# Linear attention and a bilinear layer on one core: SBUF tiles sorted into four pools by their role on TensorE

## The chip, the cores and the metric

The kernel runs on one core of a Trainium2 chip. A core has TensorE (PE, the matrix engine), VectorE (DVE), ScalarE (ACT), GpSimd (POOL) and SyncE (SP, which issues most DMAs here). SBUF is the on-chip memory of 128 partitions from which the engines read, PSUM the one that TensorE writes. The metric is the device time of one execution, in microseconds, as the median of several; less is better.

## The reference

Two stages are computed, all in float32: linear attention with positive random features, then a bilinear layer over the joined heads.

```python
scale = 1.0 / np.sqrt(np.sqrt(D))                    # 8 batches, 8 heads, 576 tokens, D = 64
def phi(x):                                          # omega: 128 features
    proj = np.einsum('bhsd,md->bhsm', x, omega)
    h = proj - np.sum(x * x, axis=-1, keepdims=True) / 2.0
    return np.exp(h - np.max(h, axis=-1, keepdims=True)) / np.sqrt(m)
q_p, k_p = phi(q * scale), phi(k * scale)
kv, z = np.einsum('bhsm,bhsd->bhmd', k_p, v), np.sum(k_p, axis=2)
num = np.einsum('bhsm,bhmd->bhsd', q_p, kv)
attn = num / (np.einsum('bhsm,bhm->bhs', q_p, z)[..., None] + 1e-06)
x = attn.transpose(0, 2, 1, 3).reshape(B * S, H * D) # 4608 tokens of 512
out = (x @ w_a) * (x @ w_b) @ w_out                  # 512 -> 1536 -> 512
```

## The kernel before

The bilinear layer's matmuls keep float32's accuracy by splitting each operand in two halves of a shorter float type (F32R), one rounded and one rest. A product of two matrices is then three matmuls for each 128 rows that are summed over: rounded by rounded, rounded by rest, rest by rounded. In one matmul one operand is *stationary* (it is loaded into the array first, by LDWEIGHTS, 128 columns) and the other *moving* (it is streamed through, 256 or 512 columns). Each matmul here has a load of its own, and the load for the next matmul is under way while the one before it streams.

The first two blocks of 512 tokens go plainly, in `moe_block`: L1319 multiplies a weight tile (stationary, names `w`, `wa`, `wb`) by x (moving, 512 columns). From block 2 on, `moe_block7` saves an eighth of the products by Strassen's scheme (Winograd's form): weights and x are added in advance (`t` tiles from DRAM, `Sa` and `Sb`), and each *unit* is seven products of six matmuls at L1410, with 256 moving columns. Their results stand in two PSUM banks `p0` and `p1`, which VectorE drains with an addition into `c` at L1420. The output matmuls are L1129 (`ghl` stationary, `wo` moving, 512 columns) and, in the last two blocks, L1198 (256 columns, with `ghl` or the sums `og` stationary and `wo` or the sums `ot` moving). The attention of the later heads runs in *bursts* between the units, as packed small fp32 matmuls: L633 (projections, `om` moving, `X` stationary), L910 (keys by values) and L982 (queries by `k`).

The order of everything is set by a planner (class `Graph`) ahead of time. It gives each buffer a *slot* of a ring; slots such as `u0` to `u11`, `x0` to `x3` or `wo0` to `wo2` are the unit of allocation, and several buffers use one slot one after another (`t` lies in `u2` to `u6`, `bq` in `a0` and `a1`, `ot` in `X0`, `X1`, `hq1` and `qd0`, `og` in `nat` and `ht` slots). The function `alloc` turns a slot into an address: it asks a pool for a tile with the slot as its tag, and the pool lays tags out one behind the other in the order in which they are first asked for.

Of the kernel before, what the change touches and what calls it, by code (L numbers as in the profile page):

```python
# [15 lines left out]
X = mybir.AxisListType.X  # L16
# [45 lines left out]
class Buf:  # L62
# [7 lines left out]
    def part(self, k):  # L70
        return self, k
# [311 lines left out]
def tile_attention_moe(ctx: ExitStack, tc: tile.TileContext, kqt, kqtt, kqn, kqnt, vx, omst, idn, wab, wout, out):  # L383
    nc = tc.nc
    SQPE = CFG["SQPE"]
    const = ctx.enter_context(tc.tile_pool(name="const", bufs=1))
    sp = ctx.enter_context(tc.tile_pool(name="sp", bufs=1))
    ps = ctx.enter_context(tc.tile_pool(name="ps", bufs=1, space=PSUM))
    dram = ctx.enter_context(tc.tile_pool(name="dram", bufs=1, space=bass.MemoryType.DRAM))
    wide = wab.dtype == I64  # L390
# [6 lines left out]
    for name, n in dict(X=2, Xw=0, nat=2, x2=0, v=1, xg=1, hk=1, hq=3, qd=1, kvz=0, sm=3, sq=3, ht=3, Xt=1, xl=0, xts=2, rd=2, x=4, xa=2, xf=2, Sa=2, Sb=2, st=0,  # L397
                        w=NF // 2, rw=0, u=NF, t=0, tst=0, wo=3, raw=2, a=2, c=0, bq=0, ghl=2, osb=0, ot=0, owr=0, og=0, ogf=0, oc=0, zs=1, z2=1, zb=2, k2=4, dn=1, tails=0, zq=2, zx=2,
# [7 lines left out]
                oc=["v0", "xg0", "Xt0", "raw0", "raw1"])  # L406
    PS = {"at", "ab", "o"}

    def alloc(b):
        pool = ps if b.ring in PS else sp  # L410
        b.ap = pool.tile(b.shape, b.dtype, tag=b.slot, name=b.name)

    def fixed(shape, dtype, name):
# [27 lines left out]
    for k in range(4):  # L441
        g.op({"POOL": 110}, lambda e, k=k: nc.gpsimd.memset(ind.ap[D * (k // 2):D * (k // 2) + D, D * (k % 2):D * (k % 2) + D], SQ2 * (k in (0, 3))),
             w=[(ind, k)], alloc=[ind] if k == 0 else [], prio=-5000)
# [55 lines left out]
    for kind, i, ws in units:  # L499
        n = place[kind, i, ws[0]]  # L500
# [1034 lines left out]
    with tc.manual_schedule():  # L1535
        for o in order:
            for b in o.alloc:
                alloc(b)
            o.fn(next(iter(o.eng)))
# [74 lines left out]
```

## Time and profile before

| | us |
|---|---|
| median of 3 runs | 1033.49 (1033.02 to 1034.39) |
| profiled execution, its own time | 1033.61 |
| its span, which the profile covers | 1031.8 |
| TensorE busy in the span | 1021.0 |
| VectorE busy | 876.7 |
| ScalarE busy | 575.5 |
| GpSimd busy | 109.1 |

The profiled execution's own time is 1.8 us longer than the span: what lies before the first and after the last instruction of the profile. Matmuls are pipelined, so a matmul's duration (281 ns in the mean for 256 columns) is far longer than the step from its start to the next one's start; the text calls that step the pace. "Busy" joins overlapping matmuls, so that a window that begins at one matmul's start and ends at a later one's start reads as busy throughout if nothing is missing between them, and its length divided by the matmuls that start in it is the pace. The count in brackets after a busy time also counts matmuls that only reach into the window.

### The profile page before, as it was taken

Reading aid. Unit: us, or ns where it says so; the run is one execution under the profiler, and the core shown is the slowest. Engines: PE = TensorE matmul, PEld = TensorE weight load, DVE = VectorE, ACT = ScalarE, POOL = GpSimd, SP = SyncE. Lnnn points to the kernel's source line nnn. Section 1 sums busy time; section 2 is a strip of 40 time slices with the busy share of each in tenths; the row PEclk is TensorE's granted clock in tenths of the full one; section 3 lists DMA queues with packets and bytes.
Section 4 is the critical chain, followed back from the end, with each engine's and each line's share of the span. In section 5 each row is a group of like instructions: output and inputs, shape, how many; then the busy total and the mean of one; then the engine's idle time right before and its main releaser. Section 6 shows DMA issues by size and latency. Waiting matters only on the chain.

```text
span 1031.8 us, 27457 instructions
## 1 busy us (share of the span) xinstructions
PE 1021.0 (99%) x10538; PEld 902.8 (87%) x10538; DVE 876.7 (85%) x2162; ACT 575.5 (56%) x1584; POOL 109.1 (11%) x157
## 2 busy tenths in 40 slices
PE   9999999999999999999999999999999999999998
PEld 7777777777798989989998988988998999999998
DVE  6999999899997979877996889888877578999776
ACT  7998897667755647655663566475454024232221
POOL 0221222101111111111110111111110000000000
PEclk9999999999999999999999999999999999999999
DMA  9778877998899988999899989988887889999991
GB/s 353 292 254 258 283 247 244 309 327 303 297 318 375 323 293 296 339 307 298 276 314 339 301 272 321 334 261 299 280 297 251 279 297 332 307 348 334 366 322 43
DMA packets 123428, 306.76 MB, mean 297 GB/s; under 512 B 17952, under 2 KB 41248, under 8 KB 123296
## 3 DMA queue, kind: packets, MB, share of 16 engines
q1 hardware_dynamic: 122416, 304.34, 86.1%
q8 instruction: 83, 1.36, 0.5%
q10 hardware_dynamic: 880, 0.66, 0.2%
q14 instruction: 49, 0.40, 0.1%
HBM read 249.60 MB, written 55.34 MB: 296 GB/s over the span
## 4 chain that ended last, share of the span: by engine, by line
PE 91%; DVE 6%; ACT 2%; issue 1%; DVEq 0%; ACTq 0%
PE p L1410 40%; PE o L1129 23%; PE pb L1319 5%; PE pa L1319 5%; PE o_P L1198 5%; PE pkv L910 3%; PE ppk L633 3%; PE p L633 2%; PE p L982 2%; DVE sm L659 1%; DVE raw L482 1%; PE p L1198 1%; PE ppq L633 1%; PE pm L982 1%; ACT hk L672 0%
## 5 line engine op out<-in xcount | busy, mean ns | idle before, releaser
L1420 DVE TENSOR_TENSOR c<-p,c 128x512 f32<-128x512 f32 (+1 forms) x336 | 208.6, 621 | 72.1 <-PE p L1410 68.4
L1129 PE MATMUL o<-wo,ghl 128*128 128x512 f32 x1008 | 258.3, 397 | 0.0
L1129 PEld LDWEIGHTS o<-wo,ghl 128*128 128x128 f32 x1008 | 181.4, 188 | 39.7 <-issue 5.0
L1410 PE MATMUL p<-x,w 128*128 128x256 f32 x1008 | 136.5, 281 | 0.2
L1410 PEld LDWEIGHTS p<-x,w 128*128 128x128 f32 x1008 | 131.0, 188 | 6.5 <-DVE c L1420 0.6
L1410 PE MATMUL p<-Sa,t 128*128 128x256 f32 x1008 | 133.1, 281 | 0.0
L1410 PEld LDWEIGHTS p<-Sa,t 128*128 128x128 f32 x1008 | 125.5, 188 | 0.1
L424 ACT COPY c<-p 128x256 f32<-128x256 f32 x84 | 31.0, 369 | 121.6 <-PE p L1410 108.5
L940 ACT ACTIVATE hq<-hq,dn 128x128 f32<-128x128 f32 x224 | 69.7, 391 | 29.2 <-DVE dn L936 28.9
L857 POOL TENSOR_TENSOR z<-hk 128x256 f32<-128x256 f32 x28 | 24.4, 870 | 532.7 <-ACT hk L672 458.9
L1410 PE MATMUL p<-x,t 128*128 128x256 f32 x504 | 73.2, 281 | 0.8 <-DVE oc L1208 0.8
L1410 PE MATMUL p<-Sb,t 128*128 128x256 f32 x504 | 73.5, 282 | 0.0
L1410 PE MATMUL p<-Sb,bq 128*128 128x256 f32 x504 | 73.3, 281 | 0.0
L930 DVE CUSTOM_DVE_ANT_0 zero<-hq,zb 128x128 bf16<-128x128 f32 x224 | 68.8, 307 | 4.1
L672 ACT ACTIVATE hq<-hq,sm 128x128 f32<-128x128 f32 x196 | 64.8, 393 | 7.4 <-DVE sm L667 7.3
L1410 PEld LDWEIGHTS p<-x,t 128*128 128x128 f32 x504 | 66.1, 188 | 2.1 <-DVE oc L1208 1.0
L672 ACT ACTIVATE hk<-hk,sm 128x128 f32<-128x128 f32 x188 | 61.3, 393 | 8.2 <-DVE sm L667 8.1
L1410 PEld LDWEIGHTS p<-Sb,t 128*128 128x128 f32 x504 | 65.7, 189 | 0.0
L1410 PEld LDWEIGHTS p<-Sb,bq 128*128 128x128 f32 x504 | 65.5, 188 | 0.1
L432 DVE TENSOR_TENSOR ghl<-c,ghl 128x512 fp32r<-128x512 f32 (+1 forms) x86 | 54.2, 643 | 5.1 <-ACT ghl L424 4.5
L424 ACT CAST ghl<-c 128x512 fp32r<-128x512 f32 (+1 forms) x60 | 32.9, 566 | 45.8 <-PE o L1129 28.0
L1470 DVE TENSOR_TENSOR c<-c,c 128x512 f32<-128x512 f32 x82 | 55.5, 711 | 0.8
(245 smaller groups left out, 1903.6 us busy)
## 6 DMA issues: line engine op xcount, KB each, us to landing
t<-td SPq DMA_DIRECT2D x168, 512.0 KB
wo<-wod SPq DMA_DIRECT2D x96, 512.0 KB
bq<-bd SPq DMA_DIRECT2D x84, 256.0 KB
qdr<-qd SPq DMA_DIRECT2D x112, 144.0 KB
hq<-qdr SPq DMA_DIRECT2D x28, 576.0 KB
X<-in_kqt_dram SPq DMA_DIRECT2D x30, 512.0 KB
td<-ts SPq DMA_DIRECT2D x24, 512.0 KB
v<-in_vx_dram SPq DMA_DIRECT2D x28, 288.0 KB
```

Source lines behind the costliest of these rows:

```text
L424: nc.scalar.copy(o(), i())
L432: return lambda e: ENG[e].tensor_tensor(o(), i(), f(hi()), op=ALU.subtract)
L633: nc.tensor.matmul(flat4(pps[w])[half, c * M:c * M + M], x()[rows, c * P:c * P + P][:, half], om.ap[rows], start=True, stop=True)
L672: g.op({"ACT": 393 if b >= B1 or not own else 359}, lambda e, c=c, w=w, to=to, at=at: nc.scalar.activation(to.ap[:, at + c], src[w](c), AF ...
L930: g.op({"DVE": 302}, lambda e, c=c, qc=qc: nc.vector.tensor_tensor_reduce(out=junk.ap[:], in0=qc(), in1=zb.ap[:], scale=1.0, scalar=0.0, o ...
L940: g.op({"ACT": 392}, lambda e, c=c, src=src: nc.scalar.activation(hq.ap[:, c], src(), AF.Copy, scale=dn.ap[:, c:c + 1]), r=[sd, (dn, None) ...
L1129: nc.tensor.matmul(po.ap[:], ghl.ap[:, gi, t * P:(t + 1) * P], wo.ap[:, wi], start=(n == 0 and i == 0), stop=(n == NF - 1 and i == 2))
L1198: nc.tensor.matmul(pb.ap[:, t], A[0](ai)[:, t * P:(t + 1) * P], W[0](wi), start=begin and t == j == 0, stop=stop and t == 1 and j == 2)
L1319: nc.tensor.matmul(pb.ap[:], wt.ap[:, wi, c], xs[c].at(xi), start=(c == 0 and i == 0), stop=(c == NC4 - 1 and i == 2))
L1410: nc.tensor.matmul(pb.ap[:, half], wcol(wi, c), xc(xi, c), start=n == 0, stop=n == 5)
L1420: g.op({"DVE": dve(n)}, lambda e: nc.vector.tensor_tensor(c4.ap[:, o], pb.ap[:, half], y(), op=ALU.add), r=[*((pb, k) for k in range(half. ...
L1470: g.op({"DVE": dve(SM)}, lambda e, v=v, C=C: nc.vector.tensor_tensor(v(C[1]), v(C[1]), v(C[0]), op=ALU.mult), r=part, w=part[2:], prio=-10)
```

## The change

One SBUF pool becomes four, and `alloc` chooses by the slot's name.

```diff
-    sp = ctx.enter_context(tc.tile_pool(name="sp", bufs=1))
+    sp = [ctx.enter_context(tc.tile_pool(name=f"sp{k}", bufs=1)) for k in range(4)]
...
+    STATIONARY, SHIM, MOVING = ("w", "u", "a", "ghl", "wo", "nat", "ht", "hk0", "hq0"), ("sm0",), ("x", "xa", "xf", "Sa", "Sb", "X", "qd", "hq1")
+
+    def part(slot):
+
+        names = (slot, slot.rstrip("0123456789"))
+        return next((k for k, part in enumerate((STATIONARY, SHIM, MOVING)) if any(n in part for n in names)), 3)
+
     def alloc(b):
-        pool = ps if b.ring in PS else sp
+        pool = ps if b.ring in PS else sp[part(b.slot)]
         b.ap = pool.tile(b.shape, b.dtype, tag=b.slot, name=b.name)
```

Pool 0 takes the slots that hold stationary operands, pool 2 those that hold moving ones, pool 3 the rest. Pool 1 holds one tile of 192 bytes, `sm0`; it stands between pools 0 and 2 and shifts the second against the first. Tiles of pools 0 and 2 are multiples of 256 bytes long, so that each pool has one offset modulo 256. The order of the instructions on every engine, the tiles that they name and the semaphores that they wait for are the same in both programs, row for row; only addresses move. Nothing is added and nothing is left out.

These are the offsets modulo 256 of the tiles that the four lines read, as both programs' allocations give them:

| slots (what lies in them) | before | now |
|---|---|---|
| `w0` to `w5` (weights) | 32, 64, 96, 128 | 64 |
| `u0` to `u11` (weights, `t`, in some blocks two of the x) | 0, 64, 128, 160, 192 | 64 |
| `a0`, `a1` (`bq`) | 32, 96 | 64 |
| `ghl0`, `ghl1` | 64, 192 | 64 |
| `wo0` to `wo2`, `hk0`, `hq0` (`wo`) | 0, 128, 160, 192 | 64 |
| `nat`, `ht` (`og`) | 0, 96, 160 | 64 |
| `x0` to `x3`, `xa0`, `xa1` | 0, 96, 128, 160, 192 | 0 |
| `Sa`, `Sb` | 128, 192 | 0 |
| `X0`, `X1`, `hq1`, `qd0` (`ot`) | 32 | 0 |
| `om` (pool `const`, moving in L633) | 192 | 192 |

A matmul's *distance* is the offset of its moving tile less that of its stationary tile, modulo 256; the parts of a tile that single matmuls read lie multiples of 256 bytes apart. By the allocations the matmuls of each line stand at these distances:

| line (matmuls in the program) | before | now |
|---|---|---|
| L1410 (3528) | 0: 732, 32: 564, 64: 468, 96: 426, 128: 396, 160: 120, 192: 444, 224: 378 | 192: 3312, 0: 216 |
| L1198 (510) | all eight, 12 to 150 each | 192: 264, 0: 246 |
| L1129 (1008) | 0: 168, 64: 336, 128: 168, 192: 336 | 0: 1008 |
| L1319 (576) | all eight, 45 to 108 each | 192: 576 |
| L633 (1080, fp32) | 160: 1008, others: 72 | 192: 896, 160: 112, 128: 72 |
| L910 (1008, fp32) | 160: 896, 224: 64, 64: 48 | 192: 1008 |

## Rows read from the trace of the kernel before

**Rows 1.** The page: its span, the busy engines, the chain by engine and line.

```profile
span 1031.8 us, 27457 instructions
...
PE 1021.0 (99%) x10538; PEld 902.8 (87%) x10538; DVE 876.7 (85%) x2162; ACT 575.5 (56%) x1584; POOL 109.1 (11%) x157
...
PE 91%; DVE 6%; ACT 2%; issue 1%; DVEq 0%; ACTq 0%
PE p L1410 40%; PE o L1129 23%; PE pb L1319 5%; PE pa L1319 5%; PE o_P L1198 5%; PE pkv L910 3%; PE ppk L633 3%; PE p L633 2%; PE p L982 2%; DVE sm L659 1%; DVE raw L482 1%; PE p L1198 1%; PE ppq L633 1%; PE pm L982 1%; ACT hk L672 0%
```

**Rows 2.** Windows of 50 us, all engines.

```profile
core 0: us, PE busy (x) PEld busy (x) DVE busy (x) ACT busy (x) POOL busy (x), PEclk, DMA share, GB/s
...
850.00:900.00 50.00, 48.98 (x387) 47.29 (x386) 45.11 (x97) 17.07 (x38) 0.00 (x0) 1.00 0.90 317
900.00:950.00 50.00, 50.00 (x426) 50.00 (x425) 47.44 (x99) 17.21 (x39) 0.00 (x0) 1.00 0.95 342
950.00:1000.00 50.00, 50.00 (x426) 50.00 (x425) 37.18 (x74) 11.15 (x29) 0.00 (x0) 1.00 0.95 347
```

**Rows 3.** Waits of PE from 200 us to the end.

```profile
PE ppq L633 <- issue: 1.5, 1, 1.5
PE p L1410 <- DVE oc L1208: 0.8, 1, 0.8
```

**Rows 4.** Windows over 114 runs of L1410, their sum.

```profile
sum 404.84, PE 404.60 PEld 403.97 DVE 334.05 ACT 188.29 POOL 37.08; mean PE 3.55 PEld 3.54 DVE 2.93 ACT 1.65 POOL 0.33
```

**Rows 5.** Windows over products of L1410, sums at distances 0, 32, 96, 192.

```profile
sum 32.87, PE 32.87 PEld 32.85 DVE 26.02 ACT 16.31 POOL 4.53; mean PE 0.71 PEld 0.71 DVE 0.57 ACT 0.35 POOL 0.10
...
sum 42.96, PE 42.96 PEld 42.93 DVE 38.91 ACT 18.23 POOL 4.37; mean PE 0.70 PEld 0.70 DVE 0.64 ACT 0.30 POOL 0.07
...
sum 38.88, PE 38.88 PEld 38.73 DVE 32.55 ACT 13.44 POOL 4.08; mean PE 0.72 PEld 0.72 DVE 0.60 ACT 0.25 POOL 0.08
...
sum 21.70, PE 21.70 PEld 21.69 DVE 17.20 ACT 8.90 POOL 1.56; mean PE 0.70 PEld 0.70 DVE 0.55 ACT 0.29 POOL 0.05
```

**Rows 6.** Fourth to sixth start in those products: distance 192, then 0.

```profile
881.93:882.16 0.24, 0.24 (x4) 0.24 (x3) 0.24 (x2) 0.00 (x0) 0.00 (x0) 1.00 1.11 443
...
958.35:958.59 0.24, 0.24 (x4) 0.24 (x3) 0.00 (x0) 0.00 (x0) 0.00 (x0) 1.00 1.15 460
...
sum 7.08, PE 7.08 PEld 7.08 DVE 5.33 ACT 2.41 POOL 0.66; mean PE 0.23 PEld 0.23 DVE 0.17 ACT 0.08 POOL 0.02
...
sum 10.99, PE 10.99 PEld 10.99 DVE 8.01 ACT 5.53 POOL 1.30; mean PE 0.24 PEld 0.24 DVE 0.17 ACT 0.12 POOL 0.03
```

**Rows 7.** Windows over three steps of L1129, sums at distances 0, 64, 128, 192.

```profile
sum 31.77, PE 31.77 PEld 25.98 DVE 25.40 ACT 15.40 POOL 3.45; mean PE 0.69 PEld 0.56 DVE 0.55 ACT 0.33 POOL 0.08
...
sum 56.81, PE 56.81 PEld 46.32 DVE 49.91 ACT 25.50 POOL 8.25; mean PE 0.69 PEld 0.56 DVE 0.61 ACT 0.31 POOL 0.10
...
sum 33.46, PE 33.46 PEld 27.14 DVE 31.54 ACT 21.73 POOL 7.57; mean PE 0.70 PEld 0.57 DVE 0.66 ACT 0.45 POOL 0.16
...
sum 66.46, PE 66.46 PEld 53.62 DVE 62.94 ACT 34.69 POOL 7.85; mean PE 0.70 PEld 0.56 DVE 0.66 ACT 0.37 POOL 0.08
```

**Rows 8.** Windows over three steps of L1319, 147 windows, all distances.

```profile
sum 102.35, PE 102.35 PEld 82.74 DVE 97.43 ACT 79.97 POOL 23.96; mean PE 0.70 PEld 0.56 DVE 0.66 ACT 0.54 POOL 0.16
```

**Rows 9.** Windows over 35 runs of L1198, their sum.

```profile
sum 55.96, PE 55.96 PEld 55.96 DVE 49.56 ACT 14.36 POOL 0.00; mean PE 1.60 PEld 1.60 DVE 1.42 ACT 0.41 POOL 0.00
```

**Rows 10.** Timeline of one drain, start and length: VectorE, then PE.

```profile
408.51 0.69 DVE L1420 TENSOR_TENSOR c<-p,c 128x512 f32<-128x512 f32 x1
...
409.72 0.87 PE L1410 MATMUL p<-x,t 128*128 128x256 f32 x6
```

**Rows 11.** Groups of instructions: VectorE differences of 128x512.

```profile
L432 DVE TENSOR_TENSOR ts<-tf,ts 128x512 fp32r<-128x512 f32 x24 | 16.1, 677 | 0.2 <-DMA td<-ts 0.2
L432 DVE TENSOR_TENSOR Sa<-st,Sa 128x512 fp32r<-128x512 f32 x14 | 10.0, 719 | 1.2 <-ACT Sa L424 1.2
```

**Rows 12.** Groups of instructions: one of L1410.

```profile
L1410 PE MATMUL p<-Sa,t 128*128 128x256 f32 x1008 | 133.1, 281 | 0.0
```

## The prediction

> **What bounds the kernel now.** I read the page first. TensorE is busy 1021.0 us of a span of 1031.8, VectorE 876.7 [rows 1]. The reader is to see that no engine but TensorE is near the span. Then the chain that ended last: the four lines of split-float matmuls (L1410, L1129, L1319, L1198) make 79% of the span, and the fp32 matmuls (L910, L633, L982) about 12% [rows 1]. [...] Last the waits of PE from 200 us to the end: two, 2.3 us in all [rows 3]. So PE is the bound because it works without a break, and the time can only fall if the break-free stream itself gets shorter: by fewer matmuls, or by a shorter pace from one matmul to the next. The change leaves every instruction, its order and its waits as they are. What is left is the pace.
>
> **What the pace depends on in this trace.** The pace is the step from one matmul's start to the next one's. Over the 114 unbroken runs of L1410 it takes 404.84 us for 3414 steps from one start to the next [rows 4]; less the 0.8 us of the one wait [rows 3] that is 118.3 ns. This is not one number. In the code each product is six matmuls; where both its pairs of tiles have the same distance (moving address minus stationary address, modulo 256, from the allocation), I put a window from its first start to the next product's start, and summed the windows by distance. There are 46, 61, 54 and 31 of them for distances 0, 32, 96 and 192; the other four distances lie between these. The sums [rows 5] divided by six times these counts give 119.1, 117.4, 120.0 and 116.7 ns. The instructions are the same in each, only the addresses differ, so the distance seems to move the pace, and 192 is the best.
>
> A product is too short to show what 192 does when it lasts: the step just before it had another distance. So I took the two steps from the fourth to the sixth start. For 192 they take 7.08 us over 31 windows, 62 steps: 114.2 ns. For 0 they take 10.99 us over 46 windows, 92 steps: 119.5 ns [rows 6]. In four of the 31 windows the two steps take 0.235 to 0.24 us (two of the four are in group 6), about 118 each; in the other 27 then (7.08 - 4 x 0.236) / 54 = 113.6. I keep this second rhythm in mind as a rival.
>
> For 512 columns I took steps of three matmuls. L1129 has 46, 82, 48 and 95 of them undisturbed, for distances 0, 64, 128 and 192: 230.2, 231.0, 232.3 and 233.2 ns, 231.9 over all [rows 7]. L1319 has 147 at 102.35 us, 232.1 ns [rows 8]. There 0 is best and 192 worst, so one distance is not best for both shapes.
>
> **The change, term by term.** By the new addresses, 3312 of the 3528 matmuls of L1410 stand at 192 and 216 at 0 (the first product of each unit in batches 3, 5 and 7, whose x lies in u slots); of L1198 264 at 192 and 246 at 0; all 1008 of L1129 at 0; all 576 of L1319 at 192.
> - L1410 at 192: 3312 x (118.3 - 114.2) = 13.6 us less. L1198 at 192: its pace now is 55.96 us over 475 steps in 35 runs, 117.8 ns [rows 9]; 264 x 3.6 = 1.0 us less.
> - Each run still has to settle. A whole product at 192 takes 116.7 a step against 114.2 in its later part, so an entry costs 6 x 2.5 = 15 ns. With 114 runs of L1410 and 36 units that start at 0 that is 150 x 15 = 2.2 us more.
> - At 0: (216 + 246) x (119.5 - 118.3) = 0.6 us more.
> - L1129: 1008 x (231.9 - 230.2) = 1.7 us less. L1319: 576 x (233.2 - 232.1) = 0.6 us more, by the row of L1129 at 192.
> - The sum of these is 14.6 - 2.2 - 0.6 + 1.7 - 0.6 = 12.9 us less.
> - Waits. A shorter PE stream meets the engines that drain its banks. A typical loop: VectorE's addition from 408.51 for 0.69 us ends at 409.20, and the product that writes this bank again starts at 409.72 [rows 10], 0.52 us later; the 12 matmuls between the bank's last product and that start take about 12 x 4.1 = 50 ns less, a tenth of this slack. The tight place is 850 to 950 us, where PE has its one wait for VectorE (L1208) and VectorE has 7.5 us free in 100. PE's 387 + 426 matmuls there, nearly all of 256 columns, get 813 x 4.1 = 3.3 us shorter, so more than half of VectorE's free time remains. I take 1 us of new waits; bounds 0 and 5 (next part).
> - At nothing: the other engines' addresses. VectorE's 128x512 differences from SBUF take 677 and 719 ns in two groups whose tiles lie at different offsets [rows 11], 6% apart at most by addresses. VectorE has 155 us free over the span [rows 1], which covers 17% on every one of its instructions; only in 850 to 950 us, with 7.5 us free, would 8% be too much, and each per cent over it costs 1 us. The fp32 matmuls: L910 goes from distance 160 to 192, L633 mostly too. No row shows them at 192. The best and the worst distance of 256 columns are 114.2 and 120.0, -3.5% to +1.4% of 118.3; on 12% of the span (124 us) that is -4.3 to +1.7 us. I take 0, inside these bounds, as no row is nearer.
>
> So 12.9 - 1 = 11.9 us less than the profiled execution's 1033.61, of which 1031.8 is the span: 1021.7. The median of the runs shown is 1033.49, 0.1 lower, so **1021.6**.
>
> [...]
>
> **The rivals.**
> - *No effect.* The distances in the trace go with tiles, and tiles with places in a unit; if the place sets the pace, new addresses change nothing: 1033.5. Against it: the 31 windows at 192 are of three kinds of product (x by w, x by t, Sb by t), lie between 294 and 992 us, and each kind has windows of 0.23 us. [...] 7%.
> - *The slow rhythm.* If the long runs lock into the rhythm of the four slow windows, 118.0 ns, L1410 gains 3312 x 0.3 = 1.0, L1198 loses 0.1, and with +1.7, -0.6 and -0.6 about 1.5 us are left: 1032. For it: four of 31, and nothing in the rows says what starts it. 8%.
> - *Another bound.* From 850 to 1000 us the DMA share is 0.90 to 0.95, and VectorE is at 95% in 900:950 [rows 2]. If nothing is gained there, 1239 matmuls x 4.1 = 5 us come back: 1026.6. Against it: PE has no wait for a DMA now [rows 3], and 3.5% on a share of 0.95 stays below 1. 7%.
> - *Slower: the fp32 matmuls.* L910 and L633 move to a distance that no row shows. It decides from 11.9 + 2.1 = 14 us, 11% on their 124 us; at 12.5% it would be 15.5 us, 1037. The whole spread over distances, 114.2 to 120.0, is 5%, so this needs twice what distance does anywhere in the trace. 6%, with whatever else new addresses may slow.
>
> **Chances and range.** The forecast has 72%. What a measurement of this kernel can tell from no change is 0.2%, 2.1 us. Faster: 72 + 7, and a little of the slow rhythm, 0.80. Same: no effect and most of the slow rhythm, 0.14. Slower 0.06. The best case has every step at 113.6 (2.1 us more), no entry cost (2.2), no new wait (1) and part of the 4.3 us on the fp32 matmuls: 1014. Upward the range takes in the other bound and the slow rhythm: 1032; no effect and slower are left out, 13%. The forecast's own range is 1015 to 1026.
>
> **What will show it.** The sums over L1410's runs: 114.5 to 115.5 ns a step instead of 118.3, and a mean of PE's 256-column matmuls under the present 281 ns [rows 12]. L1129 near 230, L1319 no better than now. PE's waits after 200 us at 2 to 4 us. Wrong would be: steps at 118 in long runs (slow rhythm), unchanged sums (no effect), more than 5 us of PE waits for VectorE or DMA (another bound), or L910 and L633 longer by more than 5 us.

## The result, and the profile after

The changed kernel takes 1024.66 us (median of four, 1024.24 to 1026.86) against 1033.94 for the kernel before beside it (1033.02 to 1036.25): a ratio of 0.9911, 95% interval 0.9889 to 0.9933, 9.3 us less. The forecast was 1021.6 with a range of 1014 to 1032, and faster at 0.80. Side and range hold; the gain is 9.3 us where 11.9 were forecast. The profiled execution took 1024.62 us, its span is 1022.7: 9.1 us less than before. Lines of the changed kernel are 7 higher: L1417 is L1410 of before, L1136 L1129, L1326 L1319, L1205 L1198, L640 L633, L917 L910.

First the page: span, busy engines, and one group of matmuls; they answer to [rows 1] and [rows 12].

```profile
span 1022.7 us, 27457 instructions
...
PE 1010.7 (99%) x10538; PEld 893.0 (87%) x10538; DVE 875.7 (86%) x2162; ACT 575.4 (56%) x1584; POOL 109.9 (11%) x157
...
L1417 PE MATMUL p<-Sa,t 128*128 128x256 f32 x1008 | 130.0, 278 | 0.0
```

The counts are those of before. PE's busy time falls by 10.3 us and VectorE's by 1.0: PE still has hardly a gap (12.0 us of the span without work, 10.8 before), and its stream has become shorter. The windows of [rows 2]:

```profile
850.00:900.00 50.00, 48.84 (x403) 47.53 (x402) 45.58 (x97) 17.05 (x37) 0.00 (x0) 1.00 0.92 323
900.00:950.00 50.00, 50.00 (x434) 49.85 (x433) 46.75 (x97) 16.15 (x37) 0.00 (x0) 1.00 0.95 345
950.00:1000.00 50.00, 50.00 (x440) 50.00 (x439) 38.67 (x77) 11.03 (x28) 0.00 (x0) 1.00 0.91 339
```

Where 1239 matmuls stood in these 150 us, 1277 stand now, at the same granted clock of 1.00. VectorE did not become the bound, and the DMA share stayed at or under 0.95. The waits of PE from 200 us on, as in [rows 3]:

```profile
PE ppq L640 <- issue: 1.5, 1, 1.5
PE p L1417 <- DVE oc L1215: 0.9, 1, 0.9
```

2.4 us against 2.3. The next rows are sums of windows over unbroken runs of one line, from a run's first start to its last. First L1417 (114 runs, 3414 steps) and L1205 (35 runs, 475 steps), to set beside [rows 4] and [rows 9]; then L1136 (130 runs, 878 steps) and L1326 (39 runs, 537 steps).

```profile
sum 397.39, PE 397.10 PEld 396.35 DVE 332.00 ACT 186.49 POOL 37.71; mean PE 3.48 PEld 3.48 DVE 2.91 ACT 1.64 POOL 0.33
...
sum 55.29, PE 55.29 PEld 55.29 DVE 49.55 ACT 14.71 POOL 0.00; mean PE 1.58 PEld 1.58 DVE 1.42 ACT 0.42 POOL 0.00
...
sum 204.77, PE 204.77 PEld 168.65 DVE 185.28 ACT 114.97 POOL 26.18; mean PE 1.58 PEld 1.30 DVE 1.43 ACT 0.88 POOL 0.20
...
sum 129.95, PE 128.98 PEld 102.93 DVE 123.76 ACT 105.47 POOL 28.16; mean PE 3.31 PEld 2.64 DVE 3.17 ACT 2.70 POOL 0.72
```

The kernel before has no row yet for the last two; the same runs there (L1129, then L1319):

```profile
sum 206.98, PE 206.98 PEld 168.83 DVE 186.79 ACT 115.35 POOL 26.39; mean PE 1.59 PEld 1.30 DVE 1.44 ACT 0.89 POOL 0.20
...
sum 128.16, PE 127.89 PEld 103.02 DVE 122.43 ACT 104.01 POOL 28.78; mean PE 3.28 PEld 2.64 DVE 3.14 ACT 2.67 POOL 0.74
```

So L1417 gains 404.84 - 397.39 = 7.45 us, L1205 0.67, L1136 2.21, and L1326 loses 1.79 (0.70 of that is idle PE: 129.95 - 128.98 against 128.16 - 127.89). Together 8.5 of the span's 9.1 us lie inside these runs; the rest lies in what is between them. L1417's mean step is 397.39 / 3414 = 116.4 ns. The prediction wanted 114.5 to 115.5.

Undisturbed steps, in windows of three as in [rows 7] and [rows 8]: L1136 in two sums of 135 windows, then L1326 in one of 146.

```profile
sum 92.75, PE 92.75 PEld 75.78 DVE 86.72 ACT 55.18 POOL 16.87; mean PE 0.69 PEld 0.56 DVE 0.64 ACT 0.41 POOL 0.12
...
sum 92.48, PE 92.48 PEld 76.20 DVE 80.62 ACT 42.19 POOL 10.70; mean PE 0.69 PEld 0.56 DVE 0.60 ACT 0.31 POOL 0.08
...
sum 102.19, PE 102.19 PEld 82.07 DVE 96.79 ACT 80.89 POOL 22.91; mean PE 0.70 PEld 0.56 DVE 0.66 ACT 0.55 POOL 0.16
```

185.23 / 810 = 228.7 ns for L1136 (231.9 before) and 102.19 / 438 = 233.3 for L1326 (232.1 before).

**Two rhythms.** To see why L1417 stays above 115.5, I cut each run of 12 or more matmuls that follows L1136 and holds no step above 126 ns (72 runs) at its tenth start, and summed what is left by two things: the distance of the run's first product, and the last step of L1136 ahead of it (the time from its last start to the run's first). The four sums: first product at 0, last step under 233 ns (17 runs, 496 steps); at 0, 233 or more (5 runs, 112 steps); at 192, under 233 (44 runs, 1012 steps); at 192, 233 or more (6 runs, 90 steps).

```profile
sum 56.22, PE 56.22 PEld 56.22 DVE 45.03 ACT 28.43 POOL 7.26; mean PE 3.31 PEld 3.31 DVE 2.65 ACT 1.67 POOL 0.43
...
sum 12.70, PE 12.70 PEld 12.70 DVE 12.31 ACT 10.59 POOL 0.50; mean PE 2.54 PEld 2.54 DVE 2.46 ACT 2.12 POOL 0.10
...
sum 118.80, PE 118.80 PEld 118.80 DVE 93.72 ACT 54.01 POOL 13.50; mean PE 2.70 PEld 2.70 DVE 2.13 ACT 1.23 POOL 0.31
...
sum 10.32, PE 10.32 PEld 10.32 DVE 9.56 ACT 5.32 POOL 3.08; mean PE 1.72 PEld 1.72 DVE 1.59 ACT 0.89 POOL 0.51
```

The quotients are 113.35, 113.4, 117.4 and 114.7 ns. Window by window there is almost nothing in between: the steps that are summed are all at distance 192, and a run goes at about 113.3 (fast) or at about 117.7 ns (slow) to its end. Twelve of these late parts, nine of them among the 44, are only two steps long. All 22 runs that start at 0 are fast. Of the 50 that start at 192, 42 are slow: 41 of 44 after a short last step of L1136, one of 6 after a long one. The slow rhythm of the prediction's rival is real. A batch is here, as in the prediction, one of the blocks of 512 tokens, counted from 0: 32 of these 42 lie in batches 2, 4 and 6, where no unit starts at 0, and the other ten, in batches 3 and 5, begin with a later product of a unit. In batch 8 no unit starts at 0 either, but its runs follow L1205 and not L1136, and they go at 55.31 us over 485 steps, 114.0 ns.

### The profile page after: what moved, and what is told of

Same layout as the page of the kernel before. It is cut to its first block, busy times and chain, and to the rows that moved or that the text cites. A ratio compares the mean times of both kernels' runs of the same rounds, so it can differ in the third digit from the quotient of the medians.

```text
span 1022.7 us, 27457 instructions
## 1 busy us (share of the span) xinstructions
PE 1010.7 (99%) x10538; PEld 893.0 (87%) x10538; DVE 875.7 (86%) x2162; ACT 575.4 (56%) x1584; POOL 109.9 (11%) x157
## 4 chain that ended last, share of the span: by engine, by line
PE 86%; DVE 8%; DMA 2%; ACT 2%; issue 1%; SPq 0%; ACTq 0%; DVEq 0%
PE p L1417 39%; PE o L1136 21%; PE o_P L1205 5%; PE pa L1326 5%; PE pb L1326 4%; PE pkv L917 3%; PE ppk L640 2%; PE p L640 2%; PE p L989 2%; DVE raw L489 1%; DVE sm L666 1%; DMA X<-in_kqt_dram 1%; PE p L1205 1%; PE ppq L640 1%; ACT hk L679 1%
## 5 line engine op out<-in xcount | busy, mean ns | idle before, releaser
L1136 PE MATMUL o<-wo,ghl 128*128 128x512 f32 x1008 | 255.5, 395 | 0.0
L1136 PEld LDWEIGHTS o<-wo,ghl 128*128 128x128 f32 x1008 | 181.0, 188 | 38.0 <-issue 4.8
L1417 PE MATMUL p<-x,w 128*128 128x256 f32 x1008 | 135.7, 281 | 0.3
L1417 PEld LDWEIGHTS p<-x,w 128*128 128x128 f32 x1008 | 130.0, 189 | 6.4 <-DVE c L1427 0.9
L1417 PE MATMUL p<-Sa,t 128*128 128x256 f32 x1008 | 130.0, 278 | 0.0
L1417 PEld LDWEIGHTS p<-Sa,t 128*128 128x128 f32 x1008 | 122.4, 188 | 0.1
L1417 PE MATMUL p<-x,t 128*128 128x256 f32 x504 | 72.6, 280 | 0.9 <-DVE oc L1215 0.9
L1417 PE MATMUL p<-Sb,bq 128*128 128x256 f32 x504 | 71.9, 279 | 0.0
L1417 PE MATMUL p<-Sb,t 128*128 128x256 f32 x504 | 71.8, 278 | 0.0
L1417 PEld LDWEIGHTS p<-x,t 128*128 128x128 f32 x504 | 65.4, 188 | 2.3 <-DVE oc L1215 1.1
L1417 PEld LDWEIGHTS p<-Sb,bq 128*128 128x128 f32 x504 | 64.5, 188 | 0.1
L1417 PEld LDWEIGHTS p<-Sb,t 128*128 128x128 f32 x504 | 64.3, 188 | 0.0
```

The costliest lines, as they stand in the source:

```text
L1136: nc.tensor.matmul(po.ap[:], ghl.ap[:, gi, t * P:(t + 1) * P], wo.ap[:, wi], start=(n == 0 and i == 0), stop=(n == NF - 1 and i == 2))
L1417: nc.tensor.matmul(pb.ap[:, half], wcol(wi, c), xc(xi, c), start=n == 0, stop=n == 5)
```

## The experiments

Twelve runs. Eleven are of the changed kernel with tiles sorted otherwise and the instructions of every engine in the same order (ten kernels, one of them run twice), one is of the changed kernel itself. The kernel before ran beside them in three groups (medians 1034.65, 1034.22 and 1034.20). "DISTANCE", "LOCK" and so on are the names of the theories in the expectations.

**Distance 0.** The 192 bytes between pools 0 and 2 are taken away.

```diff
-    STATIONARY, SHIM, MOVING = (...), ("sm0",), ("x", ...)
+    STATIONARY, SHIM, MOVING = (...), (), ("x", ...)
```

> The changed kernel without the 192 bytes between pools 0 and 2: all 3528 matmuls of L1417, all of L1205 and all 576 of L1326 stand at distance 0, L1136 stays at 0; the fp32 lines move too (L917 from 192 to 0, L640 mostly from 192 to 128). Theory DISTANCE (the pace goes with moving less stationary address modulo 256): L1417 and L1205 at 119 to 120 ns a step instead of 116.4, 4038 x 3.1 = 12.5 us more; L1326 at 229 like L1136 instead of 233.3, 576 x 4.3 = 2.5 us less; 1024.7 + 10 = 1034.7. Rival SORTING (the gain comes from tiles of one role lying together, not from the distance): 1024.7, L1417 at 116.4.

1037.11 us, ratio to before 1.0029 (1.0014 to 1.0044): about 12 us above the changed kernel, and slower than before by 0.3%. Sums over L1417's 114 runs, then over 146 windows of three steps of L1326:

```profile
sum 409.82, PE 409.65 PEld 409.01 DVE 336.53 ACT 189.32 POOL 37.50; mean PE 3.59 PEld 3.59 DVE 2.95 ACT 1.66 POOL 0.33
...
sum 99.71, PE 99.71 PEld 82.17 DVE 95.58 ACT 80.07 POOL 22.26; mean PE 0.68 PEld 0.56 DVE 0.65 ACT 0.55 POOL 0.15
```

409.82 / 3414 = 120.0 ns for L1417, and 99.71 / 438 = 227.6 for L1326. Both go the way that the distance says, in opposite directions in the one kernel. SORTING falls: tiles lie sorted by role here too, and the gain is gone. The forecast was 2.4 us low; L1417 went 0.5 ns above the 119.5 that was assumed. L1205's 35 runs take 56.99 us, 120.0 ns a step, as forecast.

**All tiles moved by 192 bytes, distances kept.** A tile of 192 bytes ahead of pool 0.

```diff
-    STATIONARY, SHIM, MOVING = ("w", ...), ("sm0",), ("x", ...)
+    FRONT, STATIONARY, SHIM, MOVING = ("sm1",), ("w", ...), ("sm0",), ("x", ...)
```

> A tile of 192 bytes ahead of pool 0: every tile of the four pools moves by 192 bytes (stationary offset 64 to 0, moving 0 to 192), all distances of the split-float lines stay; only L640, whose om lies outside the pools, goes from distance 192 to 0. Theory DISTANCE: 1024.7, within 1 us, L1417 at 116.4 and with the same slow and fast stretches. Rival ADDRESS (each tile's own offset counts, not the difference): L1417 leaves 116.4, anything up to the 118.6 of before, up to 1032. If fp32 matmuls minded their distance it would show in L640 alone.

1023.91 us (1021.70 to 1025.07), ratio 0.9899 (0.9882 to 0.9915), the same as the changed kernel's within the intervals. L1417's runs:

```profile
sum 397.61, PE 397.33 PEld 396.64 DVE 331.69 ACT 186.29 POOL 37.60; mean PE 3.49 PEld 3.48 DVE 2.91 ACT 1.63 POOL 0.33
```

397.61 against 397.39 us. ADDRESS falls as far as one such move can show it: every tile's own offset has changed, the differences have not, and the pace stays. The two rhythms come back too: cut as above, all 43 stretches of L1417 that start at 192 after a short last step are in the slow rhythm, and none of the 7 after a long one.

**The other distances.** 32, 64, 128, 160 and 224 bytes between the pools, by other small tiles in the place of `sm0`.

```diff
-    ... ("sm0",) ...
+    ... ("rd0",) ...             32 bytes
+    ... ("zq0",) ...             64
+    ... ("zx0",) ...             128
+    ... ("zx0", "rd0") ...       160
+    ... ("sm0", "rd0") ...       224
```

> The changed kernel with 64 instead of 192 bytes between pools 0 and 2: 3312 of L1417, 264 of L1205 and all of L1326 at distance 64. Theory DISTANCE with the paces that the trace of before has for it (117.6 ns at 256 columns, 231 at 512, against 115.7 and 233.3 at 192): 3576 x 1.9 = 6.8 us more, 576 x 2.3 = 1.3 us less, 1030.2. Rival: at 64 too a fast rhythm of 113.5 locks in long runs (9 of the 69 late steps of before stand there), L1417 under 116 and about 1023.

> The same with 128 bytes. Theory DISTANCE: L1417 at 119.6 ns, L1326 at 232.1: 3576 x 3.9 = 13.9 us more, 0.7 less, 1037.9. Rival: the long runs settle elsewhere than the short windows of before (113 to 123 ns were seen there), which shows in L1417's steps alone.

> The same with 32 bytes. Theory DISTANCE: L1417 at 117.4 ns, L1326 at 232.5: 3576 x 1.8 = 6.4 us more, 0.5 less, 1030.6. Rival: a fast rhythm of 113.5 in long runs, L1417 under 116 and about 1024.

> The changed kernel with 224 instead of 192 bytes between pools 0 and 2. Theory DISTANCE with the paces of before: L1417 at 118.2 ns, L1326 at 232.8; 3576 x 2.5 = 8.9 us more, 0.3 less, 1033.3. Rival: another pace in long runs, seen in L1417's steps alone.

> The same with 160 bytes. Theory DISTANCE with the paces of before: L1417 at 118.6 ns, L1326 at 233.5; 3576 x 3.0 = 10.7 us more, 0.1 more, 1035.4. Rival: another pace in long runs, seen in L1417's steps alone.

The sum over L1417's 114 runs in each of them. The kernel with 32 bytes:

```profile
sum 401.63, PE 401.41 PEld 400.75 DVE 333.00 ACT 187.01 POOL 37.64; mean PE 3.52 PEld 3.52 DVE 2.92 ACT 1.64 POOL 0.33
```

The kernel with 64 bytes:

```profile
sum 403.36, PE 403.15 PEld 402.52 DVE 333.92 ACT 187.71 POOL 37.55; mean PE 3.54 PEld 3.53 DVE 2.93 ACT 1.65 POOL 0.33
```

The kernel with 128 bytes:

```profile
sum 407.42, PE 407.22 PEld 406.57 DVE 335.26 ACT 189.20 POOL 37.66; mean PE 3.57 PEld 3.57 DVE 2.94 ACT 1.66 POOL 0.33
```

The kernel with 160 bytes:

```profile
sum 404.38, PE 404.17 PEld 403.50 DVE 335.56 ACT 186.55 POOL 37.80; mean PE 3.55 PEld 3.54 DVE 2.94 ACT 1.64 POOL 0.33
```

The kernel with 224 bytes:

```profile
sum 404.89, PE 404.68 PEld 404.03 DVE 334.65 ACT 188.99 POOL 37.76; mean PE 3.55 PEld 3.54 DVE 2.94 ACT 1.66 POOL 0.33
```

Divided by 3414 steps, beside L1326's windows of three steps worked out as above, and the times:

| distance | L1417, ns a step | L1326, ns a step | us | ratio to before |
|---|---|---|---|---|
| 0 | 120.0 | 227.6 | 1037.11 | 1.0029 (1.0014 to 1.0044) |
| 32 | 117.6 | 233.3 | 1030.87 | 0.9963 (0.9950 to 0.9975) |
| 64 | 118.1 | 229.8 | 1032.40 | 0.9983 (0.9972 to 0.9995) |
| 128 | 119.3 | 232.8 | 1036.32 | 1.0023 (1.0012 to 1.0034) |
| 160 | 118.4 | 234.1 | 1031.88 | 0.9982 (0.9970 to 0.9994) |
| 192 | 116.4 | 233.3 | 1024.66 | 0.9911 (0.9889 to 0.9933) |
| 224 | 118.6 | 233.4 | 1031.95 | 0.9983 (0.9970 to 0.9996) |

In each kernel but the first, 216 of L1417's 3528 matmuls stay at 0. DISTANCE holds, and 192 is the one distance of these seven with a large gain. The rest cannot all be ranked: the same sum in two executions of the changed kernel is 397.39 and 398.23 us, so 160 and 224, 0.5 us apart, are alike. The hoped-for fast rhythm did not lock at 32 or 64. The expectations, from short windows of before, missed by +0.3 us (32), +2.2 (64), -1.6 (128), -3.5 (160) and -1.4 (224). For 160 the pace explains it: 3.0 ns more a step than in the changed kernel were assumed, and the rows show 118.4 - 116.4 = 2.0, which over 3576 matmuls is 3.6 us. Distance 96 was not run.

**The first product at distance 0 in every batch.** `xa0` and `xa1` go to the stationary pool.

```diff
-    STATIONARY, ... = ("w", "u", "a", "ghl", ...), ..., ("x", "xa", "xf", ...)
+    STATIONARY, ... = ("w", "u", "a", "xa", "ghl", ...), ..., ("x", "xf", ...)
```

> The changed kernel with xa0 and xa1 (the x of the first product in batches 2, 4, 6 and 8) moved from pool 2 to pool 0: the first product of every unit stands at distance 0, 504 matmuls of L1417 instead of 216, all others as in the changed kernel. Theory LOCK (at distance 192 a run stays in the rhythm in which it starts, 118 or 113.5 ns; a run entered smoothly from 226.5 ns steps of L1136 starts slow, six steps at distance 0 knock it into the fast one, as in batches 3 and 7): batches 2, 4 and 6 go from 117.3 to 114.8 ns a step, 1512 x 2.5 = 3.8 us less, batch 8 pays about 0.4; 1021.3. Rival SURROUNDINGS (batches 2, 4 and 6 are slower for what runs beside them): they stay at 117 and the added steps at distance 0 cost 288 x 3 = 0.9 us, 1025.5.

1020.62 us (1020.52 to 1022.75), ratio 0.9876 (0.9859 to 0.9892); 1021.3 was expected. Sums over the runs of L1417 in batches 2, 4 and 6 (42 runs, 1470 steps), first in the changed kernel:

```profile
sum 172.73, PE 172.73 PEld 172.59 DVE 143.21 ACT 87.07 POOL 17.66; mean PE 4.11 PEld 4.11 DVE 3.41 ACT 2.07 POOL 0.42
```

The same sum in this kernel:

```profile
sum 169.30, PE 169.30 PEld 169.06 DVE 141.54 ACT 85.42 POOL 17.38; mean PE 4.03 PEld 4.03 DVE 3.37 ACT 2.03 POOL 0.41
```

117.5 ns a step becomes 115.2 (114.8 was expected): 3.43 us less, although 216 more of these matmuls stand at distance 0. In batch 8 the runs go from 55.31 to 55.68 us, 0.37 more, as LOCK forecast. The late parts here, cut as above: 45 runs that start at 0 after a short last step (1350 steps), and 16 that start at 192 after one (134 steps).

```profile
sum 153.04, PE 153.04 PEld 153.04 DVE 120.00 ACT 69.91 POOL 15.62; mean PE 3.40 PEld 3.40 DVE 2.67 ACT 1.55 POOL 0.35
...
sum 15.72, PE 15.72 PEld 15.72 DVE 13.75 ACT 5.62 POOL 3.22; mean PE 0.98 PEld 0.98 DVE 0.86 ACT 0.35 POOL 0.20
```

113.36 ns, all 45 fast; 117.3, 15 of 16 slow. The second kind begins with a later product of a unit, so the edit did not touch its start. SURROUNDINGS falls: beside the same work the same batches go fast.

**Only the second half of that product at 0.** Only `xa1` is moved.

```diff
-    STATIONARY, ... = ("w", "u", "a", "ghl", ...), ..., ("x", "xa", "xf", ...)
+    STATIONARY, ... = ("w", "u", "a", "xa1", "ghl", ...), ..., ("x", "xa0", "xf", ...)
```

> As the run with xa0 and xa1 in pool 0, but only xa1: in batches 2, 4, 6 and 8 the second three of the six matmuls of a unit's first product stand at distance 0, 360 matmuls of L1417 instead of 504, the others at 192. Theory LOCK, three steps are enough: batches 2, 4 and 6 at about 114.4 ns a step (after the full six they measured 114.6 to 115.2), 144 x 4.5 = 0.6 us less than that run's 1020.6: 1020.0. Rival LOCK, three are too few: these batches stay at 117 and the time is 1024 to 1025.

1022.12 us (1021.66 to 1022.89), ratio 0.9885 (0.9868 to 0.9901); 1020.0 was expected. Late parts of the 44 runs that start at 192 after a short last step (994 steps; the first product of many of them now has its second half at 0):

```profile
sum 113.66, PE 113.66 PEld 113.66 DVE 89.84 ACT 51.50 POOL 13.57; mean PE 2.58 PEld 2.58 DVE 2.04 ACT 1.17 POOL 0.31
```

25 of the 44 are fast, against 3 of 44 in the changed kernel. All 25 are among the 29 runs that begin a unit; the other 15 begin with a later product, which the edit did not touch, and all are slow. Three steps are often enough, not always: four of the 29, each entered after a last step of 224 ns, stayed slow. Whether this version is worse than the one with six steps the intervals leave open, as they overlap.

**L1136 at distance 192.** `wo0` to `wo2` go to the moving pool.

```diff
-    STATIONARY, ... = (..., "ghl", "wo", "nat", ...), ..., (..., "qd", "hq1")
+    STATIONARY, ... = (..., "ghl", "nat", ...), ..., (..., "qd", "hq1", "wo")
```

> The changed kernel with wo0 to wo2 in pool 2 instead of pool 0: all 1008 matmuls of L1136 go from distance 0 to 192, and 120 of L1205 too; L1417's distances stay. Theory LOCK, entry part (a run of L1417 is slow because it is entered from L1136's smooth 226.5 ns): L1136 at 233.3 instead of 229.0, 1008 x 4.3 = 4.3 us more; L1417 in batches 2, 4 and 6 mostly fast, 3 to 4 us less, L1205 0.5 less: 1024.7 to 1025. Rival (the entry does not matter): L1417 stays at 116.4 and the time is 1028.5. By DISTANCE L1136 rises to 233 in either case.

1023.20 us (1022.10 to 1024.42), ratio 0.9895 (0.9880 to 0.9909). L1136's windows of three steps in two sums of 135, as above:

```profile
sum 94.34, PE 94.34 PEld 76.19 DVE 87.78 ACT 56.61 POOL 17.35; mean PE 0.70 PEld 0.56 DVE 0.65 ACT 0.42 POOL 0.13
...
sum 94.25, PE 94.25 PEld 76.27 DVE 82.01 ACT 43.08 POOL 10.97; mean PE 0.70 PEld 0.56 DVE 0.61 ACT 0.32 POOL 0.08
```

188.59 / 810 = 232.8 ns: (232.8 - 228.7) x 1008 = 4.1 us more. Yet the kernel is not slower, since L1417's 114 runs take less, and nothing was done to their addresses:

```profile
sum 394.14, PE 393.85 PEld 393.06 DVE 329.73 ACT 185.28 POOL 37.09; mean PE 3.45 PEld 3.45 DVE 2.89 ACT 1.63 POOL 0.33
```

394.14 us instead of 397.39, as forecast (3 to 4 us less). L1205's runs go from 55.29 to 54.76, also as forecast; L1136's own go from 204.77 to 207.93, 3.2 us more where 4.3 were expected, and the time came out below the 1024.7 to 1025 of the forecast. Late parts of the runs that start at 192: 23 after a last step under 233 ns (388 steps), and 27 after one of 233 or more (720 steps).

```profile
sum 45.66, PE 45.66 PEld 45.66 DVE 33.84 ACT 17.06 POOL 3.70; mean PE 1.99 PEld 1.99 DVE 1.47 ACT 0.74 POOL 0.16
...
sum 81.60, PE 81.60 PEld 81.60 DVE 68.75 ACT 43.42 POOL 12.44; mean PE 3.02 PEld 3.02 DVE 2.55 ACT 1.61 POOL 0.46
```

117.7 ns, 22 of 23 slow; 113.3, 27 of 27 fast. L1136 alternates here between steps of 231 and 236 ns, and the rhythm of the next run goes with the step that came last. Two whole units of batch 2 in windows, the last step of L1136 and then the run from its tenth start (32 steps): the one entered at 380.45 us first.

```profile
380.21:380.45 0.24, 0.24 (x2) 0.19 (x1) 0.20 (x2) 0.00 (x0) 0.00 (x0) 1.00 0.82 312
...
381.47:385.10 3.63, 3.63 (x34) 3.63 (x33) 3.52 (x18) 1.15 (x4) 0.00 (x0) 1.00 0.93 326
```

The one entered at 392.35 us:

```profile
392.11:392.35 0.23, 0.23 (x2) 0.19 (x1) 0.23 (x1) 0.23 (x1) 0.00 (x0) 1.00 0.47 81
...
393.40:397.17 3.77, 3.77 (x34) 3.77 (x33) 3.64 (x10) 2.59 (x8) 0.00 (x0) 1.00 0.92 256
```

3.63 against 3.77 us for the same 32 steps at the same distances. The entry part of LOCK holds.

**The changed kernel and the best version once more, side by side.** No edit in the first; `xa0` and `xa1` in pool 0 in the second.

> The changed kernel unaltered, beside the version with xa0 and xa1 in pool 0 on the same chip. Theory LOCK: 1024.7, and 3 to 4 us above that version; batches 2, 4 and 6 of L1417 again at 116.9 to 117.8 ns a step and entered slow after a last step of L1136 under 233 ns. Rival CHANCE: the two differ by less than 2 us, since single executions differ by that much (a wait of 1.5 us of L640 for its instructions stands in some profiles and not in others).

> The version with xa0 and xa1 in pool 0 once more, beside the changed kernel. Theory LOCK: 1021 (1020.5 to 1021.5), batches 2, 4 and 6 at 114.6 to 115.2 ns a step. Rival CHANCE: within 2 us of the changed kernel.

1024.92 us (1024.36 to 1025.41), ratio 0.9922 (0.9908 to 0.9935), and 1021.82 us (1019.41 to 1022.37), ratio 0.9886 (0.9870 to 0.9903). The difference is 3.1 us, and the slowest execution of the second lies below the fastest of the first, so CHANCE falls; the second's own forecast of 1020.5 to 1021.5 was 0.3 us too narrow. The runs of L1417 in batches 2, 4 and 6, in the changed kernel and then in the version:

```profile
sum 172.59, PE 172.59 PEld 172.46 DVE 142.96 ACT 87.59 POOL 17.70; mean PE 4.11 PEld 4.11 DVE 3.40 ACT 2.09 POOL 0.42
...
sum 169.18, PE 169.18 PEld 168.93 DVE 141.32 ACT 85.97 POOL 17.37; mean PE 4.03 PEld 4.02 DVE 3.36 ACT 2.05 POOL 0.41
```

3.41 us less, where the first pair of executions had 3.43. Late parts again: in the changed kernel 44 runs that start at 192 after a short last step (1018 steps), in the version 45 that start at 0 after one (1362 steps).

```profile
sum 119.74, PE 119.74 PEld 119.74 DVE 94.79 ACT 52.82 POOL 14.31; mean PE 2.72 PEld 2.72 DVE 2.15 ACT 1.20 POOL 0.33
...
sum 154.41, PE 154.41 PEld 154.41 DVE 121.21 ACT 71.74 POOL 16.43; mean PE 3.43 PEld 3.43 DVE 2.69 ACT 1.59 POOL 0.37
```

117.6 ns, 43 of 44 slow, and none slow of 6 after a long last step; 113.4, all 45 fast. The version with `xa0` and `xa1` in pool 0 beats both kernels.

## Why the prediction was right in side and too large in size

**The bound and the pace.** Right. PE still works without a break, the gain lies inside the runs of split-float matmuls, and seven kernels that differ in a few bytes between two pools have paces from 116.4 to 120.0 ns. With the same instructions in the same order, distance 0 and distance 192 took 1037.11 and 1024.66 us, so on this kernel TensorE's pace is not free of where tiles lie. The runs show that the pace goes with the difference of the two addresses, not by what mechanism.

**L1410 and L1198.** Here the sum was too large. Its terms for these two lines were -13.6, -1.0, +2.2 for the entries and +0.6 at distance 0: 11.8 us less. The runs hold 3889 of the steps of their 4038 matmuls and show 8.1 us less, which scaled to all is 8.4. The term that was mis-sized is the first, 3312 x (118.3 - 114.2). The 114.2 was a mean over two rhythms in the share of the trace of before, 4 slow windows of 31. In the changed kernel 42 of 50 undisturbed runs that start at 192 behind L1136 are slow, and the late parts of all 72 runs take (56.22 + 12.70 + 118.80 + 10.32) / 1710 = 115.8 ns. Their 1710 steps alone are 1710 x 1.6 = 2.7 of the 11.8 - 8.4 = 3.4 us that were missing, and with six steps at distance 0 ahead, batches 2, 4 and 6 gain 3.43 us, net of what these steps cost. In the trace of before no stretch at 192 in L1410 is longer than 12 matmuls, so a long run at 192 was not to be seen there. The prediction's reason, that the step just before each window had another distance, is not right: by the allocation, in 17 of the 31 windows the three matmuls ahead stood at 192 as well, behind three at 128, and in four it was another line at 192. That 27 of the 31 had a step at another distance at most four matmuls ahead is the likely reason why only four windows had the slow rhythm; no run shows it. The rival of the slow rhythm stood at 8% as all or nothing, and came true in part. That the total came nearer than this term is partly luck: against 3.4 us missing here and 1.2 missing in L1319's runs stand 0.5 for L1129, 0.9 for waits and about 0.4 between the runs, all better than forecast.

One reading is off without consequence: the 120.0 ns at distance 96 holds three windows with a broken step. The other 51 give 119.1, so the worst distance of before is 128 with 119.9, and the bound that was drawn from 120.0 stays.

**L1129.** Right in sign, too small: 231.9 to 228.7 ns is 3.2 us over 1008 matmuls where 1.7 were forecast (2.2 us in the 878 steps of the runs as they are). At 0 the pace goes on falling in a long run, to steps of 226 and 227 ns from start to start, and now every run of L1136 stays at 0 from its first matmul to its last.

**L1319.** The undisturbed steps rose by 1.2 ns, 0.7 us, as forecast (0.6). The runs lost 1.79 us, with 0.70 more of idle PE in them.

**Waits.** 0.1 us instead of 1 after 200 us: the shorter stream met hardly anything that was late. Over the whole span PE's time without work rose from 10.8 to 12.0 us, most of it ahead of 200 us and 0.70 in L1326's runs; in the repeat of the changed kernel it is 11.1.

**At nothing: the fp32 matmuls, and the other engines' addresses.** Shown. VectorE's busy time fell by 1.0 us. The sum over the 28 runs (1988 steps) of L910 before, mostly at distance 160:

```profile
sum 30.23, PE 30.00 PEld 29.86 DVE 21.38 ACT 26.13 POOL 2.62; mean PE 1.07 PEld 1.07 DVE 0.76 ACT 0.93 POOL 0.09
```

Of L917 in the changed kernel, at 192:

```profile
sum 30.24, PE 30.00 PEld 29.86 DVE 21.47 ACT 26.26 POOL 3.36; mean PE 1.07 PEld 1.07 DVE 0.77 ACT 0.94 POOL 0.12
```

Of L917 in the kernel at distance 0, where it stands at 0 too:

```profile
sum 30.29, PE 30.00 PEld 29.86 DVE 21.60 ACT 25.80 POOL 3.13; mean PE 1.07 PEld 1.07 DVE 0.77 ACT 0.92 POOL 0.11
```

The sums lie within 0.06 us, and PE is busy 30.00 us in each. The 52 runs of L633, now L640, are mostly at 160 before and at 192 in the changed kernel; PE is busy 63.63 and 63.08 us in them. In the kernel with all tiles moved, where L640 is mostly at 0 and L917 and the split-float lines keep their distances, PE is busy 1011.3 us in the span, against 1010.7 in the changed kernel. The rival that had these matmuls slow down has nothing to stand on. "No effect" and "another bound" fall with the rows above; the missing 2.6 us were not lost to VectorE or a DMA.

**What stays open.** Why a difference of 192 bytes is good for 256 columns (116.4 ns a step, 120.0 at 0) and 0 for 512 (227.6 ns, 233.3 at 192), and what the two rhythms are in the hardware, no run here can show. That the rhythm goes with the last step of L1136 is shown by 27 of 27 and 22 of 23 with L1136 at 192, and with L1136 at 0 in three executions (changed kernel, its repeat, all tiles moved): 127 of 131 slow after a short step, 18 of 19 fast after a long one. Whether this step itself decides, or something that shows in it, stays open, and the exceptions are not explained.

## What to carry to other kernels

Where TensorE works back to back with a weight load for each matmul, as here, the places of tiles in SBUF are worth a sweep: put what is moving and what is stationary into pools of their own and try the bytes between them, for each shape by itself, because a distance that is good for one can be bad for another (here 192 for 256 columns, 116.4 ns a step against 120.0 at 0; and 0 for 512, 227.6 ns against 233.3 at 192). Read the pace from windows over whole runs, and by what stands ahead of each run: a mean over short windows hid here that one distance has two rhythms (in the trace of before 113.6 and about 118 ns behind a mean of 114.2). If a run can lock into the slower of two rhythms, a few steps ahead of it that cost a little can be worth more than they cost (3.1 us here).

## What was not expected of the hardware

- At distance 192 the pace of split-float matmuls of 256 columns has two values, about 113.3 and 117.7 ns, and a run mostly keeps the one it has after its first product, for some 30 steps.
- Which one it is goes with the last step ahead of the run: after 512-column steps under 233 ns (224 to 232 in the changed kernel) slow in 149 of 154 runs that start at 192 (four executions), after 233 ns or more (233 to 236 there) fast in 45 of 46. With six steps at distance 0 at their head, all 45 runs that were entered after a short step became fast (113.36 ns).
- 512 columns in L1326 went at 227.6 ns at distance 0, 229.8 at 64, and 232.8 to 234.1 at 32, 128, 160, 192 and 224; fp32 matmuls in L917 (L910 before) did not mind the distance: their 28 runs took 30.29 us at 0, 30.26 at 128, 30.23 mostly at 160 and 30.24 at 192.
